# Normalization, target updates, first sums and unit maxima at other places in a fused attention and Fourier kernel

## The chip, the cores and the metric

The kernel runs on one core of one Trainium2 chip. The metric is device time in microseconds, from the start to the end of one execution; lower is better. The kernel before takes 1979.33 us (median of three runs, 1977.02 to 1981.08).

A core has five engines with a queue each, which work at the same time and wait for each other by semaphores: TensorE (PE, matrix multiplications; its weight loads are shown as PEld), VectorE (DVE), ScalarE (ACT), GpSimd (POOL) and SyncE (SP, which here issues most DMAs). Each takes its own instructions strictly in the order in which the program gives them to it.

## The reference

The input `x` is 2048 tokens of 640 numbers. The result mixes two blocks by a gate for each token:

```python
x = A_x
g = _sigmoid((x * gate_w).sum(-1, keepdims=True))
a = _A_ref(x, A_wqkv, A_wo)          # attention, 32 heads of 20 numbers
b = _B_ref(x, B_dft_seq_re, B_dft_seq_im, B_dft_hid_re, B_dft_hid_im)
return g * a + (1 - g) * b
```

`_A_ref` is ordinary multi-head attention: queries, keys and values by `wqkv`, softmax of the scaled scores over 2048 keys, weighted values, output projection `wo`. `_B_ref` is a Fourier transform along the 640 hidden numbers and then along the 2048 tokens, of which the real part is kept: `Cr@a - Ci@b` with `a = x@Dr`, `b = x@Di`. All is in 32-bit floats, and the attention weights are large, so that the softmax needs the true maximum of each row.

## The kernel before

**Precision.** A product in full precision is made of three passes: each operand is split into a rounded part and the rest (`split`, L98 to 103), and `three` (L105) sums three of the four products.

**Ahead of the loop** (to some 270 us) queries and keys are computed and stored to memory (`qk_scr`), values too (`v_scr`), and `HEAD` = 10 blocks of the hidden transform (`hid_tile`) are done in between, each in a `segment` with four steps of score maxima.

**The attention loop.** A unit is a pair of heads and half of the queries (1024); there are 32 units, two for each head pair, and a unit has 32 steps, 1024 steps in all. One step has two "e" scores: keys by queries (matmul L682), exponential on ScalarE (L684) straight from PSUM. The exponential needs the maximum of each query's scores ahead of it. So the same scores are computed once more, queries by keys ("m", L159), `LEAD` = 41 steps ahead of the e scores; VectorE reduces each to a maximum (L161), `nm` (L167) closes a unit with one more reduction, and `max_chain` (L187) transposes the 128 x 16 maxima on TensorE, splits them into `m1` and `m2` and lets SP write them into two extra rows of the stacked queries `qst` ("rows", L198 and L199). The e matmul then subtracts the maximum by itself.

Four steps are a cycle, 256 in all. `ORDER` lists a cycle by hand: eight e, eight m, places "F" where matmuls of the Fourier part are filled in (`fill`), and one "B", the burst: weighted values (`av`, L445) of four steps, sixteen small matmuls, and after them `max_chain`, if a unit's maxima are ready. A burst begins with `run_extras`, which reads out a finished block sum and takes one or two updates whose time has come.

**Times in steps.** `at_step(i, fn)` has `fn` issue its instructions when step `i` begins. That sets a place in each engine's queue, not a time: POOL and SP run ahead of the step or behind it, as far as their waits let them. At the end of a unit (`unit_end`, step 0 of the next) ScalarE copies the weighted values to the tile `o`, of which there is one; then, at steps 1, 5, 14, 16, 20, 27 and 29, the sums are stored (`l_scr`, four DMAs), loaded in another shape, inverted on VectorE, stored, loaded as a broadcast (`rb`), `norm` on POOL (L477) multiplies, and `store_o` (four DMAs) writes the result.

Every second unit the next head pair's keys and queries (`load_stack`: four `kst` and eight `qst` loads) are issued on POOL's queue, two steps apart.

**The Fourier part** fills the places "F". First come the other 54 hidden blocks, which end at step 216; then the sequence transform, 7 products of 8 units (`PRODUCTS`, `dft_step`), in which sums and differences of quarter blocks save products. POOL prepares its operands: `load_c` (add, cast, subtract on 128 x 1024 tiles, L416, L102, L103) and `load_a` (the same on 128 x 320). A finished sum `m` (ScalarE L539, VectorE L540, two buffers) is added to or subtracted from one or two target blocks by POOL (`finish_y`: L551 if the target has been written before, L553, a multiplication by +1 or -1 into a tile `yt`, if not), and the target goes back to memory.

**Behind the loop** (from some 1889 us) the output projection runs for 16 row blocks; POOL scales the Fourier result by `1 - g` (L722) and VectorE adds the gated attention (L740).

## Time and profile before

| | |
|---|---|
| median of three runs | 1979.33 us (1977.02 to 1981.08) |
| profiled execution | 1972.39 us, its span 1970.6 us |
| granted TensorE clock, mean | 0.993 |
| TensorE busy | 98% of the span |
| VectorE, ScalarE, GpSimd busy | 74%, 62%, 56% |
| attention loop | first e matmul 270.3 us, last ends 1889.0 us |

The profiled execution's own time is 1972.39 us; its span runs from its first instruction to its last. In the rows, "idle" is time in which the engine had nothing in hand just before an instruction, and the arrow names what ended it; a wait for several things is put down to the last. Rows of the view by windows give, after the window and its length, busy time and count of PE, PEld, DVE, ACT and POOL, the granted clock, the DMA share and GB/s; where an engine has nothing in any of the windows its column is missing. Rows of the timeline give start, length, engine, line, operation and how many alike follow each other.

### The profile page before, as it was taken

The numbers are of one execution on the slowest core, as the hardware profiler recorded it, in microseconds if no ns is written. First come the engines' busy times: TensorE is split into PE (matmuls) and PEld (weight loads), VectorE is DVE, ScalarE is ACT, GpSimd is POOL, SyncE is SP. The second block draws the span as 40 slices with busy tenths as digits, with TensorE's granted clock in tenths as the row PEclk, the third lists the DMA queues.
The fourth block names the chain that finished last, engine by engine and source line by source line (L and its number), as shares of the span: only waits on it lengthen the run. The fifth ranks groups of instructions, "written<-read, shape, count | busy, mean of one in ns | idle before, by whom it ended". The sixth has DMA issues, their size and how long they took to land. (4 is left out here: it accounts for less than half of the span.)

```text
span 1970.6 us, 43800 instructions
## 1 busy us (share of the span) xinstructions
PE 1928.0 (98%) x17080; PEld 1384.3 (70%) x17080; DVE 1454.8 (74%) x2419; ACT 1212.2 (62%) x2337; POOL 1097.4 (56%) x1010
## 2 busy tenths in 40 slices
PE   8999999999999999999999999999999999999998
PEld 7987767767775666666676666666666666666678
DVE  4144569988887887888888878888888888888323
ACT  4221147767776666667776767677677666767741
POOL 1210001111004999756479987996686789787534
PEclk9999999999999999999999999999999999999999
DMA  7663321312114565436356646664555566553355
GB/s 222 172 170 132 131 91 46 84 51 72 51 51 133 181 195 161 121 111 159 101 152 191 194 151 186 195 191 125 153 175 137 172 182 184 147 169 128 102 158 177
DMA packets 196511, 281.02 MB, mean 143 GB/s; under 512 B 73373, under 2 KB 137917, under 8 KB 194385
## 3 DMA queue, kind: packets, MB, share of 16 engines
q1 hardware_dynamic: 158992, 246.20, 40.6%
q0 software_dynamic: 37312, 32.03, 6.5%
q8 instruction: 134, 2.20, 0.5%
q14 instruction: 73, 0.59, 0.1%
HBM read 213.81 MB, written 63.70 MB: 141 GB/s over the span
## 5 line engine op out<-in xcount | busy, mean ns | idle before, releaser
L161 DVE TENSOR_REDUCE mx<-ps 128x1 f32<-128x512 f32 x2048 | 1288.3, 684 | 210.4 <-PE ps L159 191.8
L684 ACT ACTIVATE p<-ps 128x512 f32<-128x512 f32 x2048 | 1081.0, 599 | 451.8 <-PE ps L159 244.4
L159 PE MATMUL ps<-kst,qst 60*128 60x512 f32 x2048 | 778.3, 428 | 19.6 <-ACT p L684 8.9
L682 PE MATMUL ps<-qst,kst 62*128 62x512 f32 x2048 | 705.2, 424 | 3.7 <-DMA qst<-m 2.2
L520 PE MATMUL yp<-a,part 64*128 64x320 f32 x5376 | 689.9, 310 | 0.1
L520 PEld LDWEIGHTS yp<-a,part 64*128 64x128 f32 x5376 | 595.2, 187 | 15.5 <-DVE m L540 0.3
L445 PE MATMUL av<-p,v 128*21 128x512 f32 x4096 | 493.3, 597 | 0.1
L682 PEld LDWEIGHTS ps<-qst,kst 62*128 62x128 f32 x2048 | 339.1, 185 | 212.6 <-DVE mx L161 179.3
L159 PEld LDWEIGHTS ps<-kst,qst 60*128 60x128 f32 x2048 | 366.0, 185 | 51.2 <-ACT p L684 12.3
L103 POOL TENSOR_TENSOR part<-raw,part 128x1024 fp32r<-128x1024 f32 x112 | 267.3, 2387 | 9.0
L445 PEld LDWEIGHTS av<-p,v 128*21 128x21 f32 x4096 | 98.2, 100 | 226.3 <-issue 222.7
L298 PE MATMUL yp<-wb,xs 64*128 64x320 f32 x1920 | 239.8, 312 | 2.1 <-ACT raw L306 1.9
L298 PEld LDWEIGHTS yp<-wb,xs 64*128 64x128 f32 x1920 | 208.9, 189 | 7.1 <-ACT raw L306 2.5
L416 POOL TENSOR_TENSOR raw<-raw,raw 128x1024 f32<-128x1024 f32 x78 | 187.8, 2408 | 9.4 <-DMA raw<-in_cdft 9.1
L551 POOL TENSOR_TENSOR yt<-yt,m 128x320 f32<-128x320 f32 x64 | 56.2, 879 | 146.9 <-DVE m L540 146.6
L102 POOL CAST wb<-raw 128x966 fp32r<-128x966 f32 (+1 forms) x4 | 3.4, 856 | 228.6 <-DMA raw<-in_wb 196.7
L102 POOL CAST part<-raw 128x1024 fp32r<-128x1024 f32 x112 | 116.3, 1039 | 18.3 <-PE yp L520 12.5
L477 POOL TENSOR_TENSOR o<-o,rb 128x512 f32<-128x512 f32 x32 | 41.5, 1296 | 133.7 <-DMA rb<-r_scr 131.5
L103 POOL TENSOR_TENSOR a<-araw,a 128x320 fp32r<-128x320 f32 x112 | 97.7, 872 | 9.0
L103 DVE TENSOR_TENSOR p<-ps,p 128x512 fp32r<-128x512 f32 x40 | 27.5, 691 | 94.9 <-ACT p L100 92.1
L106 PE MATMUL ps<-xs,part 128*128 128x512 f32 x200 | 80.3, 402 | 7.5 <-ACT xs L100 6.2
L100 ACT ACTIVATE p<-ps 128x512 fp32r<-128x512 f32 x40 | 23.8, 597 | 102.5 <-PE ps L108 102.4
(68 smaller groups left out, 1389.0 us busy)
## 6 DMA issues: line engine op xcount, KB each, us to landing
raw<-in_cdft SPq DMA_DIRECT2D x192, 512.0 KB
araw<-a_scr SPq DMA_DIRECT2D x192, 160.0 KB
qk_scr<-p SPq DMA_DIRECT2D x40, 512.0 KB
y_scr<-yt SPq DMA_DIRECT2D x96, 160.0 KB
kst<-qk_scr POOLq DMA_DIRECT2D x32, 320.0 KB, 14.1
qst<-qk_scr POOLq DMA_DIRECT2D x64, 160.0 KB, 8.7
a_scr<-raw SPq DMA_DIRECT2D x64, 160.0 KB
yt<-y_scr SPq DMA_DIRECT2D x64, 160.0 KB
```

The lines of the kernel that those rows point to most:

```text
L102: e1.tensor_copy(dst1, src)
L103: e2.tensor_tensor(dst2, src, f32(dst1), op=ALU.subtract)
L106: pe.matmul(ps, st1, mv1, start=first, stop=False)
L159: pe.matmul(ps, q[b : b + KROWS, qt * P : (qt + 1) * P], k[b : b + KROWS, kc * 512 : (kc + 1) * 512], start=True, stop=True)
L161: return lambda: dve.tensor_reduce(mx[n][:, h, qt, kc : kc + 1], ps, axis=AX.X, op=ALU.max)
L298: pe.matmul(yp[h][:, :HE], xs[r, xz, d, cs], w[r, wz, d, :HE], start=d == 0 and z == 0, stop=d == ND - 1 and z == 2)
L416: pool.tensor_tensor(raws[0], raws[0], raws[1], op=ALU.add if PRODUCTS[n][0][1][0] > 0 else ALU.subtract)
L445: pe.matmul(av[32 * j : 32 * j + DH + 1, :], v[:, kt, h * (DH + 1) : (h + 1) * (DH + 1)], pp[qc][:, h, :], start=kt == 0, stop=kt == NS - 1)
L520: pe.matmul(yp[h][:, :HE], c[r, cz, cs], a[r, az], start=s == 0 and z == 0, stop=s == NS - 1 and z == 2)
L551: pool.tensor_tensor(y, y, m, op=ALU.add if sg > 0 else ALU.subtract)
L682: pe.matmul(pt, k[b : b + KROWS + 2, kt * P : (kt + 1) * P], q[b : b + KROWS + 2, qc * 512 : (qc + 1) * 512], start=True, stop=True)
L684: act.activation(pts[n, kt, qc][:, h], pt, AF.Exp, scale=float(DH) ** -0.5)
```

## The change

- `HEAD` is 11 and `LEAD` 45.
- A unit's closing reduction `nm` is issued at the start of the burst after its last maximum; `max_chain` follows a burst later, between the two halves of that burst's `av` matmuls.
- The sums of a unit are stored by one DMA for four. The steps of normalization are 1, 4, 10, 12, 15, 23, 25.
- An update of a target block is taken five steps after its sum at the earliest (before: one), and stored four steps later (three).
- The first sum that goes to a target block is stored from `m` as it is, with its sign kept in `signs`; later sums are added or subtracted by the product of signs, and the last line of the kernel adds or subtracts the target. The first targets have no `yt` tile.
- `load_stack` issues its DMAs one and a half steps apart, `load_wb` and the first `load_c` calls have their splits placed two and four steps on. The scaling by `1 - g` has a second operand, a multiplication by 1.0.

```diff
-LEAD = 41
-HEAD = 10
+LEAD = 45
+HEAD = 11
...
         if n < NU and s == 31:
-            nms[n] = small.tile([P, 16], F32, name="nm", bufs=2)
-            dve.tensor_reduce(nms[n], mx.pop(n).rearrange("p h q c -> p (h q) c"), axis=AX.X, op=ALU.max, negate=True)
-        if s == 1 and 0 < n <= NU:
             if now[0] < 0:
-                max_chain(n - 1)
+                max_nm(n)
             else:
-                chains.append(n - 1)
+                ends.append(n)
+        if s == 1 and 0 < n <= NU and now[0] < 0:
+            max_chain(n - 1)
+
+    def max_nm(n):
+        nms[n] = small.tile([P, 16], F32, name="nm", bufs=2)
+        dve.tensor_reduce(nms[n], mx.pop(n).rearrange("p h q c -> p (h q) c"), axis=AX.X, op=ALU.max, negate=True)
...
         def store_l():
-            for j in range(4):
-                r = 32 * j + DH
-                q.dma_start(l_scr[n, j : j + 1], o[r : r + 1, :])
+            q.dma_start(l_scr[n], o.rearrange("(j r) c -> j r c", j=4)[:, DH])
...
-        steps = (1, 5, 14, 16, 20, 27, 29) if n < NU - 2 else (1, 4, 10, 12, 15, 19, 21)
+        steps = (1, 4, 10, 12, 15, 23, 25) if n < NU - 2 else (1, 4, 10, 12, 15, 19, 21)
...
             for out_, y in zip(PRODUCTS[n][2], outs.pop((n, t))):
-                extras.append((now[0] + 1, functools.partial(finish_y, out_, t, m, y)))
+                extras.append((now[0] + 5, functools.partial(finish_y, out_, t, m, y)))
...
     def finish_y(target, t, m, y):
         sg, th, hf = target
         tt = th * HT + t
-        if (tt, hf) in seen:
-            pool.tensor_tensor(y, y, m, op=ALU.add if sg > 0 else ALU.subtract)
+        if (tt, hf) in signs:
+            pool.tensor_tensor(y, y, m, op=ALU.add if sg == signs[tt, hf] else ALU.subtract)
         else:
-            pool.tensor_scalar(y, m, float(sg), None, op0=ALU.mult)
-        seen.add((tt, hf))
-        at_step(now[0] + 3, functools.partial(sp.dma_start, y_scr[tt, :, hf * HE : (hf + 1) * HE], y))
+            signs[tt, hf] = sg
+            y = m
+        at_step(now[0] + 4, functools.partial(sp.dma_start, y_scr[tt, :, hf * HE : (hf + 1) * HE], y))
...
-                    at_step(i + 2 + 2 * j, functools.partial(pool.dma_start, *args))
+                    at_step(i + 2 + 3 * j // 2, functools.partial(pool.dma_start, *args))
...
             if c + HEAD in (NS, 2 * NS):
-                load_wb(3 + (c + HEAD) // NS, pool, pool)()
+                at_step(i + 2, load_wb(3 + (c + HEAD) // NS, pool, pool))
             if c in (HID - 5, HID - 3):
-                load_c((c - HID + 5) // 2)()
+                at_step(i + 4, load_c((c - HID + 5) // 2))
...
     def burst(c):
         run_extras(max(done - HIDS, 0) // 3, 2)
-        for kt in (2 * c, 2 * c + 1):
-            av_step(now[0], kt // NS, kt % NS)
+        while ends:
+            max_nm(ends[0])
+            at_step(now[0] + 1, functools.partial(chains.append, ends.pop(0)))
+        av_step(now[0], 2 * c // NS, 2 * c % NS)
         while chains:
             max_chain(chains.pop(0))
+        av_step(now[0], (2 * c + 1) // NS, (2 * c + 1) % NS)
...
-        pool.tensor_scalar(ys[tt], ys[tt], ngate[:, tt : tt + 1], None, op0=ALU.mult)
+        pool.tensor_scalar(ys[tt], ys[tt], ngate[:, tt : tt + 1], 1.0, op0=ALU.mult, op1=ALU.mult)
...
-            dve.scalar_tensor_tensor(ye, ps, gate[:, tt : tt + 1], ye, op0=ALU.mult, op1=ALU.add)
+            dve.scalar_tensor_tensor(ye, ps, gate[:, tt : tt + 1], ye, op0=ALU.mult,
+                                     op1=ALU.add if signs[tt, hf] > 0 else ALU.subtract)
```

More of the change, by code (lines that the diff above doesn't have):

```diff
@@ L140, in q_unit @@
         return qst[n // 2 % 2][:, u : u + S // 2]
-    mx, nms, chains = {}, {}, []
+    mx, nms, ends, chains = {}, {}, [], []
     now, later = [-1], {}
@@ L494, in mix_kernel @@
     wos = {}
-    seen = set()
+    signs = {}
     outs, extras, made = {}, [], {}
@@ L504, in dft_step @@
             for _, th, hf in PRODUCTS[n][2]:
-                y = apool[0].tile([P, HE], F32, name="yt", bufs=4)
                 tt = th * HT + t
-                if (tt, hf) in seen:
+                y = None
+                if (tt, hf) in signs:
+                    y = apool[0].tile([P, HE], F32, name="yt", bufs=4)
                     sp.dma_start(y, y_scr[tt, :, hf * HE : (hf + 1) * HE])
@@ L549, in finish_y @@
         tt = th * HT + t
-        if (tt, hf) in seen:
-            pool.tensor_tensor(y, y, m, op=ALU.add if sg > 0 else ALU.subtract)
-        else:
-            pool.tensor_scalar(y, m, float(sg), None, op0=ALU.mult)
-        seen.add((tt, hf))
-        at_step(now[0] + 3, functools.partial(sp.dma_start, y_scr[tt, :, hf * HE : (hf + 1) * HE], y))
+        if (tt, hf) in signs:
+            pool.tensor_tensor(y, y, m, op=ALU.add if sg == signs[tt, hf] else ALU.subtract)
+        else:
+            signs[tt, hf] = sg
+            y = m
+        at_step(now[0] + 4, functools.partial(sp.dma_start, y_scr[tt, :, hf * HE : (hf + 1) * HE], y))
     preps = []
```

## The prediction

> **What bounds the kernel now.** I read the page first, then the idle times of TensorE (PE) by releaser, then single cycles of the attention loop, then the queues of GpSimd (POOL) and SyncE (SP) that feed them.
>
> ```profile
> PE 1928.0 (98%) x17080; PEld 1384.3 (70%) x17080; DVE 1454.8 (74%) x2419; ACT 1212.2 (62%) x2337; POOL 1097.4 (56%) x1010
> ```
>
> TensorE is busy for 98% of the span: what is to be won without removing matmuls lies in the places where it stands. These are few, and the view of waits names them (total us, times, longest; the rows left out belong to the stages ahead of the loop or behind it, or are put down to another engine):
>
> ```profile
> PE ps L159 <- ACT p L684: 8.9, 6, 3.2
> ...
> PE ps L159 <- DMA qst<-qk_scr: 4.6, 3, 2.3
> PE ps L682 <- DMA qst<-m: 2.2, 2, 1.4
> ...
> PE yp L298 <- ACT raw L306: 1.9, 2, 1.0
> ```
>
> What they cost is more than these idle microseconds, since the granted clock drops behind a long one. So I cut the loop into its 256 cycles, each from the first `av` matmul of one burst to that of the next (four steps). Thirteen cycles hold all these waits; below are some of them and their sum, then the sum over thirteen others, one for each, at the same place in a unit and in the same stage, without a wait.
>
> ```profile
> 425.02:436.39 11.37, 8.16 (x65) 6.01 (x63) 5.86 (x11) 5.19 (x10) 2.74 (x3) 0.85 0.16 45
> 600.17:608.14 7.97, 6.88 (x65) 4.61 (x63) 5.76 (x11) 4.77 (x9) 7.40 (x7) 1.00 0.16 42
> ...
> 742.09:753.11 11.02, 8.28 (x66) 5.84 (x65) 5.04 (x9) 4.81 (x9) 10.73 (x9) 0.85 0.50 157
> ...
> sum 110.64, PE 91.41 PEld 61.68 DVE 71.83 ACT 59.44 POOL 96.33; mean PE 7.03 PEld 4.74 DVE 5.53 ACT 4.57 POOL 7.41
> ```
>
> ```profile
> sum 81.45, PE 81.45 PEld 56.73 DVE 69.55 ACT 59.75 POOL 55.55; mean PE 6.27 PEld 4.36 DVE 5.35 ACT 4.60 POOL 4.27
> ```
>
> The reader is to see TensorE busy for the whole of an ordinary cycle of 6.27 us (a step is 1.57 us), and 110.64 - 81.45 = 29.2 us lost in thirteen cycles. That is all that better-placed waits can give in the loop. The `PEclk` column (0.85) shows the clock's part in the worst ones.
>
> **Why TensorE waits there.** Four chains, one example of each:
>
> ```profile
> 743.12 1.28 POOL L477 TENSOR_TENSOR o<-o,rb 128x512 f32<-128x512 f32 x1
> 744.42 1.42 SPq L485 DMA_DIRECT2D o_scr<-o  x4
> 747.23 0.60 ACT L452 ACTIVATE o<-av 128x512 f32<-128x512 f32 x1 [4.07 <-DMA o_scr<-o]
> 748.37 0.50 PE L159 MATMUL ps<-kst,qst 60*128 60x512 f32 x1 [2.75 <-ACT p L684]
> ```
>
> (B) There is one `o` tile. Its normalization (step 27) and store (step 29) leave three steps to the next unit's copy on ScalarE; if POOL is late, ScalarE waits and the exponentials behind it too. The cycles at 425.02 and 742.09 are such cases: 11.37 - 6.27 = 5.1 and 11.02 - 6.27 = 4.8 us lost.
>
> ```profile
> 1073.24 0.88 POOL L551 TENSOR_TENSOR yt<-yt,m 128x320 f32<-128x320 f32 x1 [2.07 <-DVE m L540]
> 1107.47 1.25 POOL L632 DMA_DIRECT2D kst<-qk_scr  x2
> 1131.35 0.53 POOL L632 DMA_DIRECT2D qst<-qk_scr  x1
> 1133.90 0.47 PE L159 MATMUL ps<-kst,qst 60*128 60x512 f32 x1 [1.42 <-DVE nm L167]
> 1149.01 1.28 POOL L477 TENSOR_TENSOR o<-o,rb 128x512 f32<-128x512 f32 x1
> ```
>
> (A) The maxima of a new head pair begin at step 23 (their lead of 41 counted back from 64). Their fourth `qst` load, issued by POOL at 1131.35, is just 2.5 us old there. The row names `nm`, but `nm` is long done; the load is what came last. (C) In two units the max rows (`qst<-m`) land late, because SP stood at loads whose buffers POOL had not freed. (D) Two block sums of the hidden transform wait for raw tiles (L306).
>
> A, B and C have one root: POOL runs late. Its rows:
>
> ```profile
> L103 POOL TENSOR_TENSOR part<-raw,part 128x1024 fp32r<-128x1024 f32 x112 | 267.3, 2387 | 9.0
> L416 POOL TENSOR_TENSOR raw<-raw,raw 128x1024 f32<-128x1024 f32 x78 | 187.8, 2408 | 9.4 <-DMA raw<-in_cdft 9.1 <-PE yp L520 0.2
> L551 POOL TENSOR_TENSOR yt<-yt,m 128x320 f32<-128x320 f32 x64 | 56.2, 879 | 146.9 <-DVE m L540 146.6
> L553 POOL TENSOR_SCALAR yt<-m 128x320 f32<-128x320 f32 x32 | 32.5, 1016 | 71.8 <-DVE m L540 71.6
> ```
>
> POOL waits 147 + 72 us for `m`, while it could have worked ahead, and is then short of time where the splits of the next product's `a` are added to its load.
>
> **The change, part by part.** *Target updates a burst on* (threshold +5 for +1): POOL meets `m` one burst later in its queue, so after such a wait it has up to four steps (6.3 us) of work behind it that it now has ahead. *First sums stored as they are*: 32 instructions of 1016 ns leave POOL, 32.5 us in the first three products; the store reads `m` instead (two `m` buffers, reused two units later, some 29 steps; the store goes out about 12 steps after `m`, so I cost this at nothing). The store moves to +4; SP stands less at it. *Stack loads 1.5 steps apart for 2*: the fourth `qst` load is at step 12 for 16, just as the maxima start at 19 for 23.
>
> POOL's queue for the pair above, before: from the first `kst` load to the fourth `qst` load 1131.35 - 1107.47 = 23.9 us. After, one of the two part splits (2.41 + 2.39 and a cast at under half of one, 5.8 us), one `a` split (two instructions of the shape of L551 at 0.88 and a cast at under half of that, 2.2 us) and one update of 0.88 fall behind it: 15.0 us are left, 9.6 steps. The first `kst` load itself moves from 1107.5 to about 1107.5 - 6.3 - 1.0 = 1100.2, since it follows the wait at 1073.24 and one first sum. The maxima at 1133.90, less their 1.42 us, are step 23.3, so the pair's step 0 is at 1132.5 - 23.3 x 1.57 = 1095.9, and 1100.2 is step 2.7. The fourth load is then issued at step 12.3, and needed at 19.3:
>
> ```profile
> L632 POOL DMA_DIRECT2D qst<-qk_scr x120: 509/590/729, 111.1 to 1738.7; - x120
> DMA to landing us min/median/max: 2.3/9.8/17.0
> ```
>
> The median landing of 9.8 us is 6.2 steps, so it lands at 18.5: in time, by under a step. Only a slow landing (17.0) still stalls. I take A as gone; the end on the other side is the third rival.
>
> *Normalization at 1 to 25*: the chain is store, load, reciprocal, store, load, each a little closer. `norm` moves up four steps. In the worst unit (1149.01 above, step 33) POOL comes the same 7.3 us earlier, and an `a` split, an update and a first sum (2.2 + 0.9 + 1.0) no longer stand ahead: 1137.6. Its store goes out near step 27.5, five steps ahead of the next copy. The case in the cycle of 425.02 is another one: `norm` stood behind the `wb` split at step 26 of that unit; the new order has `norm` at 23 and the split at 24. B is gone. The reciprocal at step 10 for 14 stands in VectorE's queue ahead of the maxima: its load must land by then. It is issued at 4 instead of 5, I allow it six steps (9.4 us), and the landing shown above covers that at the median; cost nothing, at worst 1 us in a few units.
>
> What is late next: `store_o` (25) now stands ahead of the max rows (26) in SP's queue, so a late `norm` would delay the rows. In that worst unit the rows would go out at 1137.6 + 1.28 + 1.42 = 1140.3, step 28.3, three steps after their place; elsewhere `norm` is earlier. I keep 1.5 us for one such stall, and for the two D cases 2.6 us (7.97 - 6.27 = 1.7 us, and half of the 1.9 us of L306's row), for nothing frees their raw tiles earlier. *One `l_scr` store for four*: three issues of 1.42/4 us saved on SP in a unit, hidden. Loop: 29.2 - 1.5 - 2.6 = 25.1 us gained, ends 8 and 29.
>
> *Maxima closed in bursts.* Three cycles tell what closing a unit costs now: an ordinary one, that with `nm`, that with the transposes; the fourth is a cycle after the last maxima.
>
> ```profile
> 336.90:343.14 6.24, 6.24 (x65) 4.43 (x63) 5.58 (x10) 4.57 (x9) 0.00 (x0) 1.00 0.09 29
> 355.61:361.98 6.37, 6.37 (x65) 4.56 (x63) 5.71 (x11) 4.63 (x10) 1.29 (x1) 1.00 0.07 26
> 361.98:368.43 6.45, 6.45 (x64) 4.48 (x64) 6.00 (x12) 4.50 (x9) 0.00 (x0) 1.00 0.12 36
> 1856.34:1861.09 4.75, 4.75 (x51) 2.90 (x49) 0.25 (x1) 4.11 (x9) 4.61 (x3) 1.00 0.21 44
> ```
>
> `nm` costs 0.13 us where it stands between maxima; in a burst VectorE has slack, so up to 31 x 0.13 = 4.0 us gained. The transpose costs 0.21, which stays; but it now splits the burst:
>
> ```profile
> 361.98 1.92 PE L445 MATMUL av<-p,v 128*21 128x512 f32 x16
> 363.82 0.28 PE L190 MATMUL ps<-ident,nm 128*16 128x128 f32 x1
> 364.03 0.50 PE L682 MATMUL ps<-qst,kst 62*128 62x512 f32 x1
> ```
>
> A change between shapes of matmul may add from nothing to the transpose's own 0.28 us a unit, 0 to 8.7 us; I take the middle, 4.3. Together about 0.3 us lost. The Trainium skill, TensorEngine Tiling (Array Packing), Key Properties, speaks against this edit: changing the tiling mode, not just the tile, drains TensorE. By that rule each unit would pay the full 0.28 and the time below would be some 4 us more; the row (0.21 us from transpose to score, less than its length of 0.28) shows no such drain behind a transpose, and the sum would then be 4 us less.
>
> *HEAD 11, LEAD 45* move one block and four steps of maxima ahead of the loop. That segment is the stretch from 246.25 to 250.54 now, 4.3 us, and covers a wait:
>
> ```profile
> 246.25 0.50 PE L159 MATMUL ps<-kst,qst 60*128 60x512 f32 x2
> 250.54 0.51 PE L106 MATMUL ps<-xs,part 128*128 128x512 f32 x1
> 262.45 0.50 PE L106 MATMUL ps<-xs,part 128*128 128x512 f32 x1 [1.31 <-ACT part L100]
> 1903.29 0.41 PE L108 MATMUL ps<-a,part 128*128 128x320 f32 x1 [1.41 <-DVE part L103]
> ```
>
> +4.3 - 1.3. In the loop one cycle of 6.24 becomes one of 4.75 (-1.5), and the transform's matmuls, about a third of a cycle, are spread over 199 cycles for 198: 0.5% of 2.1 us in some 189 cycles, 1.9 us less. Sum +3.0 - 3.4, about nothing; ends -3 and +3. *The tail*: one store for four saves POOL three issues (0.59 each by the row of `qst`) ahead of the first scaling, and the 1.41 us wait at 1903.29 goes; the scaling's second operand costs nothing or, at most, as much as two more updates of half its width, 1.8 us once at the start. I take -1.4.
>
> **The sum.** -25.1 + 0.3 + 0 - 1.4 = -26 us. The profiled execution is 1972.4 us (span 1970.6), 7 below the median of 1979.3 of the runs; the gain is a difference, so I put it on the median: 1953.3, written as 1954 us because a wait that is kept may bring a lowered clock with it.
>
> **The rivals.**
> 1. *POOL stays late.* If the update's place doesn't give the four steps, `norm` runs just four steps (6.3 us) earlier than now. The one at 743.12 then ends at 738.1, its store is out at 739.5 and SP's rows go out behind it, some 2 us ahead of the unit's first scores (just before 742.09): with a landing like the median's 9.8 they come late by up to 7 us, by about 5 in the mean of the three or so latest units. Some 16 us are given back: 1970 us. For it: POOL is full in the products that prepare an `a` of two terms; against it: 32.5 us less work and 219 us of waits to fill.
> 2. *The waits are only moved, no gain.* If TensorE made up for a wait in the cycles behind it, the 29 us would not be there: 1979 us. Against it: TensorE is busy in all 81.45 us of the thirteen ordinary cycles, so there is no room in which it could make up for one.
> 3. *Slower: the stacks are late for a lead of 45.* If POOL issues the fourth load no earlier than now, it lands near step 23.5, where the maxima wait from 19.3: 4.2 steps, 6.6 us, in each of twelve pairs. It decides from 2.2 us a pair (26/12), that is, a landing after step 20.7; with half of the pairs at 6.6 us the time is 1979 - 26 + 40 = 1993. For it: one step of slack at the median landing. Against it: the load stands four steps earlier in the queue, behind less work.
>
> **How the numbers follow.** The forecast has 0.65, rival 1 0.18, rival 2 0.05, rival 3 0.12. The predicted time is the first's; the range reaches down to all bounds met (29 + 4 + 3 us: 1946) and up to rival 1 (1971), leaving out rivals 2 and 3. Under 0.2% (4 us) a measurement of this kernel can't tell a change. Faster 0.83, same 0.05, slower 0.12.
>
> **What would show it.** Right: no `o<-av` copy waits for `o_scr<-o`, the waits of TensorE on `qst<-qk_scr` are under 2 us, `yt<-m` is gone from POOL, POOL's idle time before updates is shorter than 147 us, the cycle with `nm` is as long as its neighbours. Wrong: `qst<-m` or `qst<-qk_scr` on top of TensorE's waits, VectorE waiting for `lc<-l_scr` in the loop, or an `av` burst with a transpose that takes over 2.4 us.

## The result and the profile after

The changed kernel takes 1990.34 us (median of six runs, 1984.53 to 1996.52), the kernel before in the same session 1977.74 us (six runs, 1971.16 to 1981.08): ratio 1.0076, 95% interval 1.0049 to 1.0102. It is slower, by 12.6 us. The profiled execution of it took 1996.52 us (span 1994.7 us, mean clock 0.987), 6 us above its median; that of before lies 5 us below its own. So the two profiles differ by 24.1 us, and what follows accounts for those 24.1.

First the page, part 1, and three of its groups:

```profile
PE 1938.8 (97%) x17080; PEld 1381.9 (69%) x17080; DVE 1458.2 (73%) x2419; ACT 1211.1 (61%) x2337; POOL 1045.7 (52%) x975
...
L102 POOL CAST part<-raw 128x1024 fp32r<-128x1024 f32 x112 | 116.3, 1038 | 127.5 <-PE yp L523 88.9
L554 POOL TENSOR_TENSOR yt<-yt,m 128x320 f32<-128x320 f32 x64 | 55.3, 875 | 122.8 <-DVE m L543 122.8
L478 POOL TENSOR_TENSOR o<-o,rb 128x512 f32<-128x512 f32 x32 | 41.5, 1296 | 148.2 <-DMA rb<-r_scr 143.3
```

GpSimd has 35 instructions and 52 us less (1097.4 to 1045.7), and its idle time ahead of updates is down from 147 to 123 us. Ahead of the cast in L102 it now waits 127.5 us for buffers (18.3 before), so it is ahead of its consumers more often. The part of the change that was meant for it works. TensorE nevertheless stands more. Its waits after (total us, times, longest), the stages ahead of the loop left out:

```profile
PE ps L159 <- DVE mx L161: 31.9, 13, 5.8
...
PE yp L301 <- ACT raw L309: 5.4, 2, 4.4
...
PE ps L159 <- ACT p L687: 0.8, 3, 0.3
PE ps L159 <- DMA qst<-qk_scr: 0.7, 1, 0.7
```

The waits shown of before are gone or nearly so: behind the `o` tile 8.9 us became 0.8, on `qst<-qk_scr` 4.6 became 0.7, on the max rows 2.2 became nothing. One row has grown from 2.0 us in 3 waits to 31.9 us in 13, more than all of them had: TensorE waits for VectorE to take a maximum out of PSUM. VectorE itself waits, in the same view for its engine, for one small load:

```profile
DVE lc L468 <- DMA lc<-l_scr: 39.2, 11, 8.9
```

Ten of the eleven lie in the loop (the other is the last unit's, behind it). One of them, in the timeline of VectorE and then of TensorE (start, length, engine, line; in brackets the idle time before and what ended it):

```profile
702.45 1.29 DVE L161 TENSOR_REDUCE mx<-ps 128x1 f32<-128x512 f32 x2 [0.37 <-PE ps L159]
709.13 0.25 DVE L468 RECIPROCAL lc<-lc 128x16 f32<-128x16 f32 x1 [5.39 <-DMA lc<-l_scr]
709.30 1.22 DVE L161 TENSOR_REDUCE mx<-ps 128x1 f32<-128x512 f32 x2
```

```profile
709.99 0.79 PE L159 MATMUL ps<-kst,qst 60*128 60x512 f32 x1 [5.31 <-DVE mx L161]
712.63 3.15 PE L448 MATMUL av<-p,v 128*21 128x512 f32 x16
715.71 0.50 PE L685 MATMUL ps<-qst,kst 62*128 62x512 f32 x1
```

The reciprocal of a 128 x 16 tile takes 0.25 us. But it stands in VectorE's queue at step 10, ahead of the maxima; until its load lands, 5.39 us, no maximum is taken, the PSUM buffers stay full, and TensorE stands 5.31 us. The burst behind it takes 3.15 us for 16 matmuls, and 1.91 us in the undisturbed cycle at 757.57; the granted clock of its cycle is 0.83 for 1.00. Cut into cycles, this is what such a wait costs; of fifteen cycles some, and their sum, then the first two of fifteen undisturbed ones at the same places, and their sum (view by windows; the columns as in the prediction):

```profile
700.04:712.63 12.59, 7.28 (x59) 4.92 (x57) 6.23 (x13) 4.53 (x9) 4.62 (x8) 0.83 0.71 187
712.63:719.96 7.33, 7.33 (x59) 4.25 (x57) 4.35 (x8) 4.18 (x8) 7.12 (x6) 0.83 0.66 196
907.89:919.93 12.04, 7.28 (x58) 4.93 (x56) 6.23 (x13) 4.53 (x9) 4.01 (x5) 0.86 0.65 141
919.93:927.71 7.78, 7.78 (x58) 4.26 (x57) 4.35 (x8) 4.18 (x8) 6.62 (x10) 0.78 0.58 149
...
1538.60:1546.42 7.82, 6.34 (x58) 4.16 (x56) 5.58 (x11) 4.57 (x10) 5.10 (x4) 1.00 0.71 185
1640.00:1647.46 7.46, 6.35 (x57) 4.19 (x56) 5.15 (x10) 4.23 (x9) 5.04 (x9) 1.00 0.77 194
...
1749.52:1757.26 7.74, 7.74 (x57) 4.34 (x56) 4.95 (x9) 4.11 (x9) 6.55 (x7) 0.79 0.53 125
sum 136.50, PE 107.31 PEld 67.20 DVE 79.13 ACT 64.53 POOL 86.73; mean PE 7.15 PEld 4.48 DVE 5.28 ACT 4.30 POOL 5.78
```

```profile
757.57:763.74 6.17, 6.17 (x59) 4.17 (x57) 5.06 (x10) 4.24 (x9) 5.88 (x7) 1.00 0.16 54
763.74:769.83 6.09, 6.09 (x57) 4.11 (x56) 4.97 (x9) 4.13 (x8) 5.80 (x6) 1.00 0.99 312
...
sum 92.04, PE 92.04 PEld 62.16 DVE 76.93 ACT 63.91 POOL 62.70; mean PE 6.14 PEld 4.14 DVE 5.13 ACT 4.26 POOL 4.18
```

136.50 - 92.04 = 44.5 us, of which 31.9 at most is idle time; the rest is matmuls at a granted clock of about 0.8, in the cycle with the wait and, whole, in the next one (7.33 us for 6.09). Two more cycles, where block sums of the hidden transform wait for raw tiles, cost 20.70 - 12.50 = 8.2 us:

```profile
585.52:598.19 12.67, 8.30 (x64) 5.99 (x62) 5.65 (x10) 4.88 (x9) 2.73 (x2) 0.87 0.51 140
610.67:618.70 8.03, 6.89 (x64) 4.63 (x63) 5.66 (x10) 4.75 (x9) 7.38 (x6) 1.00 0.27 67
sum 20.70, PE 15.19 PEld 10.62 DVE 11.31 ACT 9.63 POOL 10.11; mean PE 7.59 PEld 5.31 DVE 5.65 ACT 4.82 POOL 5.05
```

```profile
sum 12.50, PE 12.50 PEld 8.86 DVE 11.15 ACT 9.14 POOL 1.28; mean PE 6.25 PEld 4.43 DVE 5.58 ACT 4.57 POOL 0.64
```

So the change took away its 29 us of waits and put about 53 us in their place.

**Which units.** The ten waits all follow an odd unit (7, 9, 11, 13, 15, 17, 21, 23, 25, 27) and stand near step 12 of the even unit behind it. Steps 2 to 18 of an even unit are where GpSimd issues the next head pair's keys and queries. The packets of the small load, in the trace, say the same: 128 packets of 64 bytes, the last of which ends 1.2 to 4.2 us after the issue behind even units, and 8.2 to 15.8 us behind those ten odd ones. Most of the packets aren't late there: in all ten, 96 of the 128 have ended 1.3 to 6.4 us after the issue, and it is the last quarter that the reciprocal waits for. In the trace of before the load was slow too (up to 12.8 us behind odd units), under the cover of a reciprocal at step 14.

### The profile page after: what moved, and what is told of

The parts are those of the page before. It is cut to its first block, busy times and chain, and to the rows that moved or that the text cites. A ratio compares the mean times of both kernels' runs of the same rounds, so it can differ in the third digit from the quotient of the medians.

```text
span 1994.7 us, 43688 instructions
## 1 busy us (share of the span) xinstructions
PE 1938.8 (97%) x17080; PEld 1381.9 (69%) x17080; DVE 1458.2 (73%) x2419; ACT 1211.1 (61%) x2337; POOL 1045.7 (52%) x975
## 5 line engine op out<-in xcount | busy, mean ns | idle before, releaser
L159 PE MATMUL ps<-kst,qst 60*128 60x512 f32 x2048 | 780.0, 430 | 35.4 <-DVE mx L161 31.9
L448 PE MATMUL av<-p,v 128*21 128x512 f32 x4096 | 506.6, 606 | 0.1
L419 POOL TENSOR_TENSOR raw<-raw,raw 128x1024 f32<-128x1024 f32 x78 | 187.7, 2406 | 15.2 <-DMA raw<-in_cdft 13.4
L102 POOL CAST part<-raw 128x1024 fp32r<-128x1024 f32 x112 | 116.3, 1038 | 127.5 <-PE yp L523 88.9
L102 POOL CAST wb<-raw 128x966 fp32r<-128x966 f32 (+1 forms) x4 | 3.4, 852 | 201.4 <-PE ps L159 190.1
L103 DVE TENSOR_TENSOR p<-ps,p 128x512 fp32r<-128x512 f32 x40 | 27.5, 691 | 92.5 <-ACT p L100 89.7
```

The costliest lines, as they stand in the source:

```text
L102: e1.tensor_copy(dst1, src)
L103: e2.tensor_tensor(dst2, src, f32(dst1), op=ALU.subtract)
L159: pe.matmul(ps, q[b : b + KROWS, qt * P : (qt + 1) * P], k[b : b + KROWS, kc * 512 : (kc + 1) * 512], start=True, stop=True)
L419: pool.tensor_tensor(raws[0], raws[0], raws[1], op=ALU.add if PRODUCTS[n][0][1][0] > 0 else ALU.subtract)
L448: pe.matmul(av[32 * j : 32 * j + DH + 1, :], v[:, kt, h * (DH + 1) : (h + 1) * (DH + 1)], pp[qc][:, h, :], start=kt == 0, stop=kt == NS - 1)
```

## The experiments

To compare them, each kernel's loop was cut into its cycles; its **excess** is the sum, over all cycles that are more than 0.6 us longer than the median of those at the same place of a unit in the same stage, of what they are longer. This is worked out from the trace of one execution.

| kernel | median us | ratio to before (95%) | span of the profile | excess | span less excess |
|---|---|---|---|---|---|
| before | 1977.7 | | 1970.6 | 28.5 | 1942.1 |
| after | 1990.3 | 1.0076 (1.0049 to 1.0102) | 1994.7 | 53.4 | 1941.3 |
| e1_recip14 | 1964.2 | 0.9949 (0.9930 to 0.9968) | 1969.7 | 26.1 | 1943.6 |
| b1_recip10 | 1982.7 | 1.0034 (1.0020 to 1.0049) | 1981.2 | 38.4 | 1942.8 |
| e2_nostack | 1944.3 (one run) | | 1942.5 | 0 | 1942.5 |
| e3_nov | 1991.5 (one run) | | 1989.7 | 45.7 | 1944.0 |
| e4_store27 | 1959.9 | 0.9927 (0.9911 to 0.9942) | 1958.5 | 15.0 | 1943.5 |
| e5_three | 1961.2 | 0.9938 (0.9922 to 0.9955) | 1958.8 | 18.7 | 1940.1 |
| e6_loadc | 1988.4 (one run) | | 1986.6 | 46.1 | 1940.5 |
| b2_norm | 1966.7 | 0.9969 (0.9954 to 0.9983) | 1966.7 | 25.0 | 1941.7 |
| e10_apart2 | 1991.1 | 1.0077 (1.0054 to 1.0101) | 1991.2 | 47.8 | 1943.4 |
| e7_best | 1958.1 | 0.9916 (0.9894 to 0.9938) | 1961.6 | 19.6 | 1942.0 |
| e8_stack1 | 1947.2 | 0.9858 (0.9838 to 0.9878) | 1944.2 | 7.1 | 1937.1 |
| e9_lead41 | 1977.6 | 1.0012 (1.0001 to 1.0023) | 1975.7 | 17.1 | 1958.6 |

The last column is the main finding in one place: but for the last two rows, what these kernels differ by stands, to within 4 us, in a few long cycles. (The runs of before shared by each group had medians of 1975.0 us for the first four experiments, 1973.3 for the next four and 1975.6 for the last four.)

### The reciprocal's place

The theory: the reciprocal at step 10 waits for a load that is late. The rival: something else in the new order delays VectorE, and the reciprocal only stands where it shows. One kernel moves it back in the changed kernel, one moves it forward in the kernel before.

```diff
-        steps = (1, 4, 10, 12, 15, 23, 25) if n < NU - 2 else (1, 4, 10, 12, 15, 19, 21)
+        steps = (1, 4, 14, 15, 18, 23, 25) if n < NU - 2 else (1, 4, 10, 12, 15, 19, 21)
```

> The changed kernel with the reciprocal at step 14 instead of 10 (the store at 15 and the loads at 18 behind it; norm stays at 23, the store of o at 25). Theory 1: the new waits of TensorE at step 12 of every second unit come from VectorE, which stands at the reciprocal until the load of the sums has landed (near step 11.5); with step 14 the 44 us of those cycles go, VectorE's wait for lc falls from 39 us to under 3, and the time is 1950 us (1944 to 1958). Theory 2: the waits come from the longer lead or from the maxima closed in bursts, and the reciprocal only stands where VectorE stops anyway: the waits stay within 10 us of the 32 us shown, the time is 1985 to 1992.

```diff
-        steps = (1, 5, 14, 16, 20, 27, 29) if n < NU - 2 else (1, 4, 10, 12, 15, 19, 21)
+        steps = (1, 5, 10, 16, 20, 27, 29) if n < NU - 2 else (1, 4, 10, 12, 15, 19, 21)
```

> The kernel before with the reciprocal alone moved from step 14 to step 10. Theory 1: the packets of the lc load end at steps 11.2, 11.1, 11.5 and 12.4 in four units of the kernel before, so TensorE gets four new waits there, 6 to 12 us with the clock; 1984 to 1990 us, and VectorE waits 6 to 12 us for lc. Theory 2: no new waits, since nothing else is moved: 1978 us.

Measured: with the reciprocal at 14 the changed kernel takes 1964.2 us, ratio 0.9949. Three numbers take away 26 us, and the change is a gain, though not the 1950 us that the first theory expected. TensorE's waits in it:

```profile
PE ps L685 <- DMA qst<-m: 6.9, 3, 3.1
...
PE ps L159 <- DMA qst<-qk_scr: 5.0, 1, 5.0
PE yp L301 <- ACT raw L309: 4.0, 2, 3.8
```

The wait on the maxima is gone from the loop; of 44.5 us some 17 come back in other places (the excess falls by 27.3, from 53.4 to 26.1). By its cycles, the 26.1 us are 11.5 at the max rows, 7.6 at the stacks (unit 20) and 7.0 at the raw tiles. The first row is new: the max rows are late, three times. One of them, GpSimd and SP, then TensorE:

```profile
730.62 1.29 POOL L478 TENSOR_TENSOR o<-o,rb 128x512 f32<-128x512 f32 x1
731.93 1.41 SPq L486 DMA_DIRECT2D o_scr<-o  x4
734.34 0.66 SPq L201 DMA_DIRECT2D qst<-m  x1
739.76 0.59 PE L685 MATMUL ps<-qst,kst 62*128 62x512 f32 x2 [1.77 <-DMA qst<-m]
```

That is the first rival's mechanism: `norm` is late (at step 27.5 in this unit), SP stands at `store_o` for it, and the rows wait behind.

In the kernel before, the reciprocal at 10 costs far less, ratio 1.0034: VectorE waits there four times, 14.4 us with the last unit's, and not eleven times and 39.2. The 1982.7 us lie just under the first theory's 1984 to 1990. So the place alone doesn't make the loss. Something in the changed kernel makes the load later, too.

### What makes the load late

Two transfers overlap it: the keys and queries (GpSimd's queue), and the next values (336 KB, and not the 1.4 MB that the expectation below gives; on SP's queue as the load itself, issued just behind it). Two kernels leave out the one and the other from the third head pair on; the heads then reuse what an earlier pair left, and only the time is of use.

```diff
-                for j, args in enumerate(load_stack(p + 1)):
+                for j, args in enumerate(load_stack(p + 1) if p < 1 else ()):
```

> The changed kernel without the loads of keys and queries for the head pairs after the second (the maxima and scores of later pairs use old operands; this work is left out, so the output differs). If the stack loads of POOL's queue hold up the load of the sums: it lands within 4 us of its issue in every unit, VectorE doesn't wait for it, no wait at step 12, about 1945 us. If the loads of the weighted values' operand or the queue of SP hold it up: the landing stays at 10 to 15 us in units 7, 11, 15, 17 and 23, and the time at 1980 to 1990.

```diff
+        if p > 1:
+            vts[p] = vts[p - 2]
+            return
```

> The changed kernel without the loads of v for the head pairs after the second (older values are used; this load is left out, so the output differs). If the stack loads hold up the load of the sums: the landings stay late, 10 to 15 us after issue in units 7, 11, 15, 17, 23, and TensorE's waits for VectorE stay above 20 us. If the v load does (1.4 MB in the same queue, in the same units): the landings are within 4 us and the waits go.

Measured: without the stack loads 1944.3 us, an excess of 0, and one single wait on the load, the last unit's. Without the values 1991.5 us, like the changed kernel itself. VectorE's row in the one and in the other:

```profile
DVE lc L468 <- DMA lc<-l_scr: 9.8, 1, 9.8
```

```profile
DVE lc L471 <- DMA lc<-l_scr: 34.2, 9, 8.7
```

The values aren't the cause: without them nine of the eleven waits are left. The stack loads are needed for it. Leaving them out takes away both their transfers and their instructions on GpSimd; that it is the transfers is read from the DMA view of the stretch around the wait above (690 to 710 us), first the changed kernel, then the one without stack loads in its like stretch (684 to 704 us):

```profile
DMA  1039499889998999999987597799455444321389
GB/s 49 33 83 132 180 262 262 205 221 262 238 245 216 327 396 335 259 289 322 260 118 109 93 205 115 239 209 160 115 184 169 125 120 133 95 65 59 75 257 315
DMA packets 2652, 3.77 MB, mean 188 GB/s; under 512 B 1269, under 2 KB 2021, under 8 KB 2557
...
q1 hardware_dynamic: 1457, 2.49, 48.4%
q0 software_dynamic: 1194, 1.27, 27.9%
```

```profile
DMA  0006989988999999999999510000012994558888
GB/s 0 0 16 115 319 311 385 352 254 303 352 369 392 363 393 384 399 336 367 408 401 418 213 41 25 0 0 0 0 17 69 297 342 128 185 119 310 307 230 277
DMA packets 2817, 4.60 MB, mean 230 GB/s; under 512 B 609, under 2 KB 2043, under 8 KB 2815
...
q1 hardware_dynamic: 2815, 4.56, 67.3%
```

Each digit is the mean busy share of the 16 DMA engines in half a microsecond, in tenths; the row below is what they moved. q0 holds the stack loads, q1 those that SP issues. Without stack loads the engines are full from 685.5 us on, move 250 to 420 GB/s from 686 us, and are done after some 10 us. With them there are more than 15 us of transfer; from 700 to 709 us 60 to 240 GB/s are moved, with the engines busy for five to nine tenths up to 704 us and five or less behind that, so not all of the 16 have work all the time. SP itself stands then: a pair of its issues (`araw<-a_scr`, from 702.03) takes 6.23 us in the changed kernel, and 1.85 us (from 688.63) in the other. In the trace's packets, q0's bytes come in 94 packets of 8192 bytes, 530 ns each in the mean, and 120 of 4096, 238 ns; a 64-byte packet of the small load takes 11 ns. The small load isn't long, then; its last packets come to their turn late. The Trainium skill, DMA: Bandwidth & Descriptors, Issuing engines are not separate DMA queues, says that DMAs started by different engines run on the same 16 DMA engines and interleave. These rows agree in so far as packets of both queues run in the same 20 us and SP's transfers take longer beside the others. In what order an engine takes the packets of two queues, and how the stack loads' packets lie on the 16 engines, stays open: the trace doesn't name a packet's engine.

SP's own loads seem to belong to the cause as well. In units 1 and 3, in the hidden stage, the stack loads move 0.55 and 0.67 MB while the small load is under way and SP's queue under 0.5 MB, and it lands after 5.7 and 6.4 us. In e2_nostack SP's queue alone moves up to 1.7 MB in that time, and it lands after 5.1 us at most. The ten landings of 8.2 us and more have both, 0.56 to 1.2 MB and 1.2 to 2.4 MB. No run takes these loads of SP's queue away (e3_nov leaves out 336 KB of them), so this isn't tested.

The last piece, the spacing of the stack loads:

```diff
-                    at_step(i + 2 + 3 * j // 2, functools.partial(pool.dma_start, *args))
+                    at_step(i + 2 + 2 * j, functools.partial(pool.dma_start, *args))
```

> The changed kernel with its stack loads two steps apart again, as before; reciprocal at step 10 as in the changed kernel. In before with the reciprocal at 10, VectorE waited for lc only 4 times in the loop (14.4 us); in the changed kernel 11 times (39.2 us). Theory 1 (the closer stack loads also made the small load slower): the waits of VectorE for lc fall to 15 to 22 us in 4 to 7 waits and the time to about 1975 us. Theory 2 (spacing is nothing, the rest of the new order brings the stack loads and the small load together): the waits stay at 35 us or more and the time at 1985 to 1995 us; the fourth query load, issued two steps or more later, may add 2 to 8 us of waits on qst<-qk_scr.

Measured: VectorE's waits fall as the first theory has it,

```profile
DVE lc L468 <- DMA lc<-l_scr: 14.9, 5, 8.8
```

which is the number of the kernel before with its reciprocal at 10 (14.4). So, in VectorE's waits, the closer loads make up the difference between the two. The landings themselves move less. In the ten units the median landing is 12.2 us after the issue in the changed kernel, 10.1 us here, and 7.9 us in b1_recip10. The small load still isn't fast, but it lands at steps 8.0 to 11.3 and not at 9.5 to 11.6, and a landing ahead of the reciprocal's turn costs nothing. The rest of the lateness, 10.1 against 7.9 us, may come from another part of the new order (with LEAD and HEAD back as well, in e9_lead41 below, the median is 7.3); no run singles it out. The time does not fall (1991.1 us, for 1975 expected), since the other wait takes the place:

```profile
PE ps L159 <- DMA qst<-qk_scr: 17.0, 4, 8.1
PE ps L159 <- DVE mx L161: 8.7, 7, 2.6
...
PE ps L159 <- issue: 5.6, 2, 3.4
```

Four times the fourth `qst` load is late for the lead of 45, at step 20 of an even unit, and twice more at that same step a wait that the profile puts down to nothing; the fourth load lands just then in these two as well (steps 19.7 and 19.6). I had allowed 2 to 8 us for it; it is 17, and 22.6 with the two. Here a closer spacing spares the lead and costs the small load: neither of the two spacings tried with the reciprocal at 10 gives a gain.

### What else the normalization costs

```diff
-        steps = (1, 4, 10, 12, 15, 23, 25) if n < NU - 2 else (1, 4, 10, 12, 15, 19, 21)
+        steps = (1, 4, 14, 15, 18, 23, 27) if n < NU - 2 else (1, 4, 10, 12, 15, 19, 21)
```

> The changed kernel with the reciprocal at 14, its store at 15, the loads at 18, norm at 23 and the store of o at step 27, behind the max rows (26) in SP's queue instead of ahead of them (25). Theory 1: the three waits of the max rows that came up with the reciprocal at 14 (1.8 + 3.1 + 2.0 us at the first step of units 9, 17 and 19) go, since norm ends by step 29 and the next copy needs o at 33; 1955 us (1950 to 1960). Theory 2: the rows are late because SP stands at other loads: two or three of these waits stay, 1962 to 1966 us.

The same seven steps in the kernel before:

> The kernel before with the normalization alone at steps 1, 4, 14, 15, 18, 23 and 27 (one step of it after another place, the reciprocal left at 14). Theory 1: the o tile is free in time in all units, so the three waits at step 2 (3.2, 2.7 and 2.0 us, 13 us with the clock) go and the waits for the stack loads stay: 1962 us (1958 to 1967). Theory 2: POOL is late at norm whatever its step, and two of the three waits stay: 1970 to 1975 us.

Measured: 1959.9 us in the changed kernel, ratio 0.9927; the three waits for max rows are gone, as `store_o` now stands behind them in SP's queue. In the kernel before, 1966.7 us, ratio 0.9969: the steps alone take away most of the wait behind the `o` tile (3.1 us are left of 8.9 in that row), and leave that on the stacks (8.2 us of idle time there, 4.6 before). The rest of the change is thus worth some 0.4% on top of the steps (0.9927 against 0.9969, with intervals that don't meet).

### The early operands and the transposes

Two parts of the change were left to test: `load_c`, whose splits come four steps later, and the transposes between the two halves of a burst.

```diff
-                at_step(i + 4, load_c((c - HID + 5) // 2))
+                load_c((c - HID + 5) // 2)()
```

> The changed kernel with the splits of the first two transform loads issued at once again, as before the change, and nothing else. Theory 1: one or two key loads instead of four are ahead of the transform's load, and the store of the block sum lands earlier: the wait of 4.4 us on L309 falls to 1 us or less. Theory 2: the wait stays at 4 us.

With this, the steps of e4_store27, and the transposes behind both halves:

```diff
-        av_step(now[0], 2 * c // NS, 2 * c % NS)
+        for kt in (2 * c, 2 * c + 1):
+            av_step(now[0], kt // NS, kt % NS)
         while chains:
             max_chain(chains.pop(0))
-        av_step(now[0], (2 * c + 1) // NS, (2 * c + 1) % NS)
```

> The kernel of the run before, with two more parts of the change undone: the first two transform loads have their splits issued at once again, and the transposes stand behind both halves of the burst. Theory 1 (four key loads issued at once, together with the transform's first load, hold up the store of a block sum): the wait of 3.8 to 4.4 us at the first product's loads falls to 1 us or less, 6 us gained; the cycle with the transposes falls from 6.58 to 6.45 us, 31 x 0.13 = 4 us gained; together 1945 us (1940 to 1951). Theory 2: the splits' place in POOL's queue is of no weight and the transposes cost the same in both places: 1955 us.

The same without the `load_c` edit:

> The changed kernel with the reciprocal at step 14, the normalization at 23, the store of o at 27, and the transposes behind both halves of a burst instead of between them. Against the same without the last edit (1959.9 us): if a transpose between the halves costs what its cycle shows (6.578 against 6.455 us), 31 units by 0.12 us give 4 us: 1956 us, with the nm cycle unchanged at 6.24. If the split costs nothing, 1960 us.

Measured: with `load_c` at once the wait for raw tiles falls from 5.4 to 1.2 us in the changed kernel, and a new one of 6.2 us on `qst<-qk_scr` comes, at step 20 of unit 6: the stack loads stand behind the split in GpSimd's queue. The time, 1988.4 us in one run, is within the changed kernel's own runs; in e5_three (1961.2 us) the same trade is seen. It moves a wait of one pair, and no gain shows: the two cycles together take 22.1 us (8.20 + 13.90) for 20.7. e5_three reaches neither the 1945 us nor the 1955 us of its theories: its raw tiles wait only 1.3 us, but `qst<-qk_scr` 11.7 us, at units 6 and 20.

The transposes' own cost shows in the cycles, here that of one unit in the hidden stage: in the changed kernel the cycle with `nm` and the one with the transposes between the halves, then in e7_best the one with the transposes behind them:

```profile
358.66:364.89 6.23, 6.23 (x64) 4.43 (x62) 5.70 (x11) 4.57 (x9) 0.00 (x0) 1.00 0.19 53
364.89:371.47 6.58, 6.58 (x65) 4.40 (x63) 6.04 (x12) 4.57 (x9) 0.00 (x0) 1.00 0.09 30
```

```profile
368.45:374.89 6.44, 6.44 (x66) 4.48 (x64) 6.01 (x12) 4.57 (x9) 0.00 (x0) 1.00 0.12 36
```

0.14 us a unit, 4.3 us in 31. The times, 1958.1 against 1959.9 us, have intervals that overlap: the profile of e7_best has a stall of its own (15.54 us for one cycle ahead of unit 20, below). In time it isn't settled.

### The spacing and the lead

Both start from e7_best. One sets the stack loads one step apart, the other undoes LEAD, HEAD and the spacing together.

```diff
-                    at_step(i + 2 + 3 * j // 2, functools.partial(pool.dma_start, *args))
+                    at_step(i + 2 + j, functools.partial(pool.dma_start, *args))
```

> As the kernel before it in this list, with the stack loads one step apart. If the last wait on qst<-qk_scr (5.2 us, the pair before unit 20's step 20) is only a matter of where POOL issues the fourth load, it goes and the time is 1950 us. If closer loads slow the small load of lc or each other, VectorE's waits for lc come back although the reciprocal is at 14 (they were gone) or the maxima rows come late, and the time is 1960 us or more.

```diff
-LEAD = 45
-HEAD = 11
+LEAD = 41
+HEAD = 10
...
-                    at_step(i + 2 + 3 * j // 2, functools.partial(pool.dma_start, *args))
+                    at_step(i + 2 + 2 * j, functools.partial(pool.dma_start, *args))
```

> As the second kernel of this list, with LEAD 41, HEAD 10 and the stack loads two steps apart, all as before. If the longer lead with its blocks moved ahead is worth about nothing, as the prediction has it (+3.0 in the prologue, -3.4 in the loop), and the need of the stacks moves as much as their fourth load, the time is 1956 us like the second kernel, within 4 us; the loop then begins 3 us earlier. If lead 45 costs in earnest, 1950 us; if it was the lead that took the stack waits away, waits on qst<-qk_scr of 5 us or more come back and the time is 1963 us or more.

Measured: one step apart gives 1947.2 us, ratio 0.9858, the fastest complete kernel here. The wait ahead of unit 20 (one cycle each, e7_best and then e8_stack1) is nearly gone, and the reciprocal at step 14 covers the small load even so (VectorE has one wait for it, the last unit's):

```profile
1315.00:1330.54 15.54, 7.27 (x57) 4.93 (x56) 5.65 (x11) 4.14 (x8) 15.25 (x15) 0.77 0.76 187
```

```profile
1307.12:1314.98 7.86, 6.30 (x57) 4.17 (x56) 4.99 (x9) 4.24 (x9) 4.95 (x7) 1.00 0.61 151
```

Lead 41 gives 1977.6 us, and not the 1956 of "worth nothing" nor, with one wait of 4.0 us on them, the 1963 of the stacks. What comes back is neither theory's wait:

```profile
PE ps L685 <- DMA qst<-m: 17.8, 27, 3.1
PE ps L159 <- DMA qst<-qk_scr: 4.0, 1, 4.0
```

The e scores wait 27 times for their max rows. Closing a unit in bursts puts the transposes a burst later, and with a lead of 41 the rows land in `qst` after the unit has begun. The cycle with the transposes takes 7.03 us there, and 6.44 us in e7_best (above), where it comes one cycle earlier in the unit: about 0.6 us in 27 units, 16 us. As this is in nearly every unit, the median holds it too, and the table's excess does not: 1958.6 - 16 comes to 1942.6, like the others. So the longer lead is the price of the bursts, and not an extra. The one-step spacing, for its part, isn't harder on the small load than the one and a half steps of the changed kernel (the median landing in the ten units is 12.4 us for 12.2, the latest 13.4 for 15.8): denser loads made it later from two steps to one and a half, and no further.

## Why the prediction was wrong

**The step that failed** is the reciprocal at step 10: "It is issued at 4 instead of 5, I allow it six steps (9.4 us), and the landing shown above covers that at the median; cost nothing, at worst 1 us in a few units". The landing shown was that of the `qst` loads, another load on another queue, and its median of 9.8 us is over the 9.4 allowed even so. The runs show 1.2 to 4.2 us behind even units and up to 15.8 us behind odd ones, landings as late as step 11.6, ten waits in the loop and 44.5 us in all. The median of an unlike load was taken for a bound; and where the load's landing wasn't in a row, the trace's packets of before had it (up to 12.8 us). The move was also looked at alone, though the same change pushes the stack loads, the transfer that slows it, closer together: b1_recip10 and e10_apart2 put VectorE's waits at 14 to 15 us without that, and the changed kernel has 39.2 with it (some 9 of each are the last unit's).

**The sum.** In the profiled executions the forecast is 1970.6 - 26 = 1944.6 us of span, and the changed kernel has 1994.7: 50.1 us missed. The reciprocal is 44.5 of them and the raw tiles 8.2 - 2.6 = 5.6; the stall of 1.5 us kept for the max rows didn't come. That is 48.6. In the medians the miss is smaller, 26 + 12.6 = 38.6 us, as the one profile lies above its median and the other below. The span of e2_nostack, where no wait of the loop is left and the stack loads are left out, is 1942.5 us.

The reciprocal isn't the whole of it. With it back at 14 (e1_recip14) the gain is 0.5%, some 10 us of the 26: the prediction kept 1.5 us for the max rows, 2.6 for the raw tiles and none for the stacks, and they cost 11.5, 7.0 and 7.6 us there. The range has a slip besides: 1979 less 29 + 4 + 3 us is 1943, and not 1946.

Point by point:

- *A, stacks late*: gone, as forecast (0.7 us of idle time for 4.6). For the pair whose queue was worked out, the fourth load goes out at step 11.2 of the trace, for 12.3. It was tight, though: in four kernels with the reciprocal at 14 (e1, e4, e5, e7) one pair still waits 5 us or more at unit 20, and with loads two steps apart (e10) four do.
- *B, one `o` tile*: gone, in part by luck in the working. `norm` of the unit worked out is at step 23.9, where the prediction had 26.5, but TensorE's new stall ahead of it (5.5 us, or 3.5 steps, in its two cycles) gave GpSimd that time: with the reciprocal at 14 (e1_recip14) the same `norm` is at step 28.0. Even so the profile has no copy there that waits for `o_scr<-o`.
- *C, max rows*: 1.5 us allowed, none came, behind the same stalls; with the reciprocal at 14 and `store_o` still at 25 it did, 6.9 us of idle time (e1_recip14).
- *D, raw tiles*: mis-sized, 2.6 us forecast, 8.2 measured. The splits of `load_c` four steps later were listed and never priced; e6_loadc shows that they make it.
- *Bursts*: right in both terms, as far as the hidden stage shows them. The medians over it: the cycle with `nm` fell from 6.364 to 6.236 us (-0.13, forecast -0.13), that with the transposes rose from 6.450 to 6.578 (+0.13; the middle of 0 and 0.28 was taken, 0.14). The second hit is luck: a middle was taken for want of a row. The Trainium skill, TensorEngine Tiling (Array Packing), Key Properties, says that a change of tiling mode drains TensorE. It gives no time for that, and no run here shows whether these matmuls differ in mode; of the 0.28 us that the prediction set for it, half is measured.
- *HEAD and LEAD*: the first e matmul comes at 273.27 us for 270.28, +2.99 (forecast +3.0; in the other kernels with 11 blocks it comes at 271.2 to 276.3, in those with 10 at 270.1 to 271.2, so that the match is this close by luck). That the lead is worth nothing otherwise was wrong in the reason: e9_lead41 shows that the bursts need it.
- *Tail*: from the last e matmul to the end 78.8 us (1994.7 - 1915.9) for 81.6, -2.8 (forecast -1.4).
- *Rivals*: in the changed kernel GpSimd was not late, and the stacks were not late; the slower outcome came by a mechanism that stood only among the signs of a wrong prediction ("VectorE waiting for `lc<-l_scr` in the loop"). The first rival's wait is real, but waited behind this one: it shows as soon as the reciprocal is moved back.

## What to carry to other kernels

An instruction that waits for a load holds up all that stands behind it in its engine's queue: before it is moved ahead, take the landing of that very load, in the worst unit and beside whatever else will be in transfer then, not a median of another. When a plan closes several gaps at once, look for the pair of edits that meet in one resource; here the reciprocal's load had less time and the loads beside it were made denser. And test a losing change part by part: three numbers turned 1.0076 into 0.9949, and three edits together (four of the seven steps, the transposes back behind the burst, the stack loads one step apart) into 0.9858.

## What the runs showed of the hardware

- A load of 8 KB in 128 packets of 64 bytes has its last packet 1.2 us after the issue when nothing else is in transfer (behind unit 16 of the changed kernel), and 8.2 to 15.8 us after it in ten units in which key and query loads of the other queue run beside those of its own; around one of these they move 1.3 MB in 20 us. Without the key and query loads, and with its own queue as it was, it takes 1.2 to 5.1 us in every unit of the loop (e2_nostack).
- A wait of TensorE of 5.3 us cost 7.7 us: its cycle and the next take 12.59 + 7.33 us for 6.17 + 6.09, at a granted clock of 0.83 in both. The two cycles of 7.82 and 7.46 us, with waits of 1.5 and 1.1 us in them, kept a clock of 1.00 and cost 1.7 and 1.3 us. A wait of 2.1 us (in the cycle from 1434.99 us) had clocks of 0.90 and 0.88 in its cycle and the next.
- Without its long cycles the kernel takes much the same time in these versions: the span less the excess is 1940 to 1944 us in twelve of them, although the order of much that runs off TensorE differs between before and after.
